# Exponents of split 64-bit weights: one ScalarE operation in place of two, in an attention and MLP kernel

## The chip, the cores and the metric

The kernel runs on one core of one Trainium2 chip. A core has a matrix engine (TensorE, PE in the profile, with its weight loads shown apart as PEld), a vector engine (VectorE, DVE), a scalar engine (ScalarE, ACT), a general engine (GpSimd, POOL), and a sync engine (SP) whose queue issues most of the transfers. Each engine works through its own instructions in a fixed order; semaphores hold an instruction until what it needs is done. The metric is the device time of one execution in microseconds (us); less is better.

## The reference

Sixty-four attention heads (8 batches of 8) with a sequence of 576 and a head size of 64, in which each query keeps only its 32 largest scores, followed by a layer of two matrix products with `h - tanh(h)` between them:

```python
scores = scale * np.matmul(q, k.transpose(0, 1, 3, 2))
kth = np.partition(scores, -top_k, axis=-1)[..., -top_k:-top_k + 1]
scores = np.where(scores >= kth, scores, -1000000000.0)
scores = scores - np.max(scores, axis=-1, keepdims=True)
attn = np.exp(scores)
attn = attn / (np.sum(attn, axis=-1, keepdims=True) + 1e-09)
attn_out = np.matmul(attn, v)
x = attn_out.transpose(0, 2, 1, 3).reshape(B * S, H * D)   # 4608 x 512
h = x @ w_in                                               # w_in 512 x 2048
g = h - np.tanh(h)
out = g @ w_out                                            # w_out 2048 x 512
```

`q`, `k` and `v` are 32-bit floats. `w_in` and `w_out` are 64-bit floats, since they come from a division by a 64-bit number. No engine computes with these, so the kernel turns their bits into 32-bit floats itself.

## The kernel before

**Attention.** The work is a list of 144 steps; a step is 128 queries of a pair of heads. Four stages of successive steps overlap. For step n+1, PE makes the scores (line 238) and ACT copies them out of PSUM (line 246). For step n, DVE searches for the 32 largest: it forms pairwise minima and maxima (lines 268, 269), takes the eight largest of the minima (line 271), and then runs four rounds of MAX8 (line 276) and MATCH_REPLACE8 (line 279). For step n-1, POOL forms the threshold (line 295), ACT turns it into a mask (line 308, once for each head), POOL subtracts the mask (line 311, a tensor operation of 128x576 twice in each step), marks doubtful rows (line 315), and ACT takes exponentials (line 331). For step n-2 the weights are transposed, multiplied with `v` by PE (lines 436, 444), copied by ACT (line 448) and scaled by POOL (line 460). In the first batch, PE transposes them (line 412) and ACT copies the result (line 415); in later batches DVE and transfers through DRAM do.

**The layer.** When all heads of 256 rows (128 in some units) are there, PE forms `h` (line 489), ACT takes tanh and a copy (lines 501, 502), POOL subtracts (line 503), and PE multiplies by `w_out` (line 510). This work is dealt out between the attention steps.

**The weights.** `w_in` and `w_out` are cut into 32 pieces of 128 x 512 numbers. A piece is brought in twice by SP (lines 148 and 149: the raw words, and the same bytes shifted so that the mantissa lies in one word), and then goes through the engines:

- DVE line 158 takes the 11 bits of the exponent out of the high word, into the tile `f`, as an integer;
- ACT lines 159 and 162 turn them into the bits of a 32-bit exponent, `e`;
- DVE line 164 and ACT line 167 turn the mantissa into a number from 1 to 2, in the tile of the weights;
- DVE line 170 joins sign and exponent into `f`;
- POOL line 173 multiplies the two.

The steps of the generator `convert` are spread over the four search rounds of the first eleven attention steps, two to four pieces in a step (`many`). A stretch of the trace in which a step's search and its pieces run is called a round in what follows. In each, line 170 of a piece comes after lines 158 and 164 of the next one on DVE. For the pieces of `w_in` (the first 16) `e` is a tile in PSUM; for those of `w_out` it is `f` itself, in SBUF:

```python
e = h_ps.tile([P, NW], FP32, tag="h", name="e")[:] if j < WJ else f[:]
```

The room in which a piece is loaded is partly borrowed (from `w_out`, from `spare`, from `zx`), so a new load starts when line 170 of an earlier piece has read its slot. The order on each engine is the order in which the program issues (`tc.manual_schedule()`); nothing moves it later.

Of the kernel before, what the change touches and what calls it, by code (L numbers as in the profile page):

```python
# [8 lines left out]
AF = mybir.ActivationFunctionType  # L9
ALU = mybir.AluOpType  # L10
FP32 = mybir.dt.float32
I32 = mybir.dt.int32
# [36 lines left out]
def kernel(  # L49
# [9 lines left out]
    nc = tc.nc  # L59
    P = nc.NUM_PARTITIONS  # L60
# [16 lines left out]
    scale = 1.0 / float(D) ** 0.5  # L77
# [5 lines left out]
    def pool(name, bufs, **kw):  # L83
        return ctx.enter_context(tc.tile_pool(name=name, bufs=bufs, **kw))

    consts = pool("consts", 1)
# [28 lines left out]
    later = spare[:].rearrange("p a n w -> p (a n w)").bitcast(FP32)  # L115
    zx2 = [consts.tile([P, 4 * S], FP32, name="zx")[:], later[:, 0 : 4 * S]]
    et_rem = later[:, 4 * S : 6 * S]
    e1151 = consts.tile([P, 1], FP32, name="e1151")
    nc.gpsimd.memset(e1151[:], 1151.0 * 2.0**23)
    e255 = consts.tile([P, 1], FP32, name="e255")  # L120
    nc.gpsimd.memset(e255[:], 255.0 * 2.0**23)

    def flat(x):
        return x.rearrange("p n w -> p (n w)")
# [13 lines left out]
    def convert(piece, slot):  # L138


        j, i = piece // CD, piece % CD
        if j < WJ:
            src, dst = moe_w_in[i * P : (i + 1) * P, j * NW : (j + 1) * NW], w_in[j][:, i, :]
        else:
            r0 = ((j - WJ) * FJ + i) * P
            src, dst = moe_w_out[r0 : r0 + P, :], w_out[j - WJ][:, i, :]
        raw, shifted, _ = slot
        nc.sync.dma_start(flat(raw), src.bitcast(U32))
        nc.sync.dma_start(
            flat(shifted).bitcast(U8)[:, 0 : 8 * NW - 4], src.bitcast(U8)[:, 3 : 8 * NW - 1]  # L150
        )
        yield
        hi = raw[:, :, 1]
        f = thpool.tile([P, NW], FP32, tag="th", name="f")
        fu = f[:].bitcast(U32)


        nc.vector.tensor_scalar(fu, hi, 20, 0x7FF, ALU.logical_shift_right, ALU.bitwise_and)
        nc.scalar.activation(f[:], fu, AF.Relu, bias=e1151[:], scale=-(2.0**23))  # L159

        e = h_ps.tile([P, NW], FP32, tag="h", name="e")[:] if j < WJ else f[:]
        nc.scalar.activation(e.bitcast(I32), f[:], AF.Relu, bias=e255[:], scale=-1.0)

        nc.vector.tensor_scalar(
            dst.bitcast(U32), shifted[:, :, 0], 0x0FFFFFFF, None, ALU.bitwise_and
        )
        nc.scalar.activation(dst, dst.bitcast(U32), AF.Copy, bias=1.0, scale=2.0**-28)
        yield

        nc.vector.scalar_tensor_tensor(  # L170
            out=fu, in0=hi, scalar=0x80000000, in1=e.bitcast(U32), op0=ALU.bitwise_and, op1=ALU.bitwise_or
        )
        nc.gpsimd.tensor_tensor(dst, dst, f[:], ALU.mult)
        yield
# [398 lines left out]
    def run(exact):  # L573
# [32 lines left out]
        def load_piece():  # L606
            k = len(loaded)
            usable = [x for x in free if x[2] > k]
            if k < pieces and usable:
                slot = min(usable, key=lambda x: x[2])  # L610
                free.remove(slot)
                piece = convert(k, slot)
                next(piece)
                loaded.append((piece, slot))
# [161 lines left out]
```

## Time and profile before

| | us |
|---|---|
| median of 3 runs | 1538.54 (1538.29 to 1539.8) |
| profiled execution | 1541.86 |
| its span, first to last instruction | 1540.1 |

Busy time in the profiled execution: PE 1441.5 us (94%), DVE 1346.9 (87%), POOL 940.9 (61%), ACT 883.4 (57%). The chain of work that ended last lies on PE for 79% of the span, on DVE for 7%, on ACT for 4%. The 32 conversions run between 8.2 and 166.4 us; PE is not yet full there.

The views of the profile give one line for a group of like instructions, or, in order of time, one line for an instruction or a run of them: start, duration, engine, line of the program, operation, the tile written and the tiles read, the shape, and in brackets how long the engine had been idle before and what ended that. A duration runs from start to end, so it holds what the instruction waits for once it has started. The granted clock is the share of TensorE's full clock that the chip allowed.

### The profile page before, as it was taken

What the parts mean: (1) busy time and instruction counts of PE and PEld (TensorE: products, weight loads), DVE (VectorE), ACT (ScalarE), POOL (GpSimd) and SP (SyncE); (2) the same over time, 40 slices, a digit from 0 to 9 for tenths busy, and PEclk for the clock granted to TensorE, in tenths of its full rate; (3) what the DMA queues carried; (4) which work ended last, traced back from release to release, by engine and by line L of the source; (5) the groups of instructions that cost most, each with busy time, mean ns of one, the idle gap of its engine ahead of it and who ended that gap; (6) DMA issues with size and microseconds to landing.
All of it is one profiled execution on the core that took longest, in us unless ns stands there. A gap on an engine that the chain in (4) does not pass through costs nothing.

```text
span 1540.1 us, 24174 instructions
## 1 busy us (share of the span) xinstructions
PE 1441.5 (94%) x7428; PEld 911.6 (59%) x7428; DVE 1346.9 (87%) x3828; ACT 883.4 (57%) x1567; POOL 940.9 (61%) x1525
## 2 busy tenths in 40 slices
PE   2567898999999999999999999999999999999997
PEld 1355566556566665656566665656566665656673
DVE  6988899999999999999999999999999999997300
ACT  4887776556555565556565565656565565655320
POOL 2777677567575675757575675757575675746420
PEclk9887999999999999999999999999999999999999
DMA  9944114546754575446655565456655566534400
GB/s 233 367 168 172 50 32 102 143 130 176 173 157 137 146 168 161 127 141 154 177 136 146 146 161 160 128 149 154 172 136 149 146 153 165 147 114 116 137 7 16
DMA packets 255466, 221.61 MB, mean 144 GB/s; under 512 B 197728, under 2 KB 204896, under 8 KB 248160
## 3 DMA queue, kind: packets, MB, share of 16 engines
q1 hardware_dynamic: 253552, 219.75, 53.1%
q8 instruction: 61, 1.00, 0.3%
q14 instruction: 77, 0.63, 0.2%
q10 hardware_dynamic: 1776, 0.22, 0.1%
HBM read 136.17 MB, written 83.76 MB: 143 GB/s over the span
## 4 chain that ended last, share of the span: by engine, by line
PE 79%; DVE 7%; ACT 4%; DMA 3%; issue 2%; SPq 2%; POOL 2%; DVEq 0%; ACTq 0%; POOLq 0%
PE hps L489 30%; PE ops L510 29%; PE av L436 10%; PE scps L238 9%; DVE m L276 2%; DVE ab L279 2%; PE av L444 2%; SPq L201 1%; DMA et<-there 1%; ACT z L308 1%; ACT f L159 1%; PE zt L412 1%; DMA zx<-in_moe_w_in_dram 1%; DVE ab L268 1%; DVE ab L271 1%
## 5 line engine op out<-in xcount | busy, mean ns | idle before, releaser
L510 PE MATMUL ops<-w_out,g 128*128 128x512 f32 x1152 | 520.5, 598 | 0.0
L489 PE MATMUL hps<-xT,w_in 128*128 128x256 f32 (+1 forms) x2176 | 471.4, 372 | 1.2 <-POOL xT L460 1.2
L276 DVE MAX8 m<-ab 128x8 f32<-128x288 f32 (+1 forms) x1152 | 464.1, 444 | 0.0
L311 POOL TENSOR_TENSOR z<-sc,z 128x576 f32<-128x576 f32 x288 | 400.2, 1412 | 77.1 <-ACT z L308 77.1
L489 PEld LDWEIGHTS hps<-xT,w_in 128*128 128x128 f32 x2176 | 390.7, 193 | 73.9 <-issue 20.7
L279 DVE MATCH_REPLACE8 ab<-m,ab 128x288 f32<-128x288 f32 x864 | 376.0, 443 | 0.0
L510 PEld LDWEIGHTS ops<-w_out,g 128*128 128x128 f32 x1152 | 211.4, 191 | 244.7 <-issue 240.7
L308 ACT ACTIVATE z<-sc,tb 128x576 f32<-128x576 f32 x288 | 207.6, 769 | 153.8 <-POOL tb L295 153.8
L503 POOL TENSOR_TENSOR g<-g,th 128x512 f32<-128x512 f32 x144 | 183.8, 1276 | 123.5 <-ACT g L502 109.0
L331 ACT ACTIVATE z<-z,nb 128x576 f32<-128x576 f32 x288 | 221.6, 773 | 8.7 <-POOL z L311 8.6
L246 ACT COPY sc<-scps 128x1152 f32<-128x1152 f32 x144 | 160.8, 1116 | 108.5 <-PE scps L238 106.4
L238 PE MATMUL scps<-kT,qT 64*128 64x288 f32 (+1 forms) x1280 | 188.1, 445 | 30.2 <-DVE qT L223 27.7
L238 PEld LDWEIGHTS scps<-kT,qT 64*128 64x128 f32 (+1 forms) x1280 | 101.4, 184 | 118.9 <-issue 56.4
L436 PE MATMUL av<-et,vb 128*64 128x256 f32 (+1 forms) x1088 | 133.3, 381 | 38.4 <-ACT et L415 30.6
L268 DVE TENSOR_TENSOR ab<-scps,sc 128x576 f32<-128x576 f32 x144 | 107.6, 747 | 68.0 <-POOL bad L315 55.0
L460 POOL TENSOR_TENSOR xT<-xs 128x256 f32<-128x256 f32 (+1 forms) x68 | 47.2, 695 | 168.0 <-ACT xs L448 168.0
L501 ACT ACTIVATE th<-hps 128x512 f32<-128x512 f32 x144 | 85.4, 593 | 106.8 <-PE hps L489 104.4
L448 ACT COPY xs<-av 128x512 f32<-128x512 f32 (+1 forms) x84 | 44.1, 525 | 169.6 <-PE av L444 169.6
L436 PEld LDWEIGHTS av<-et,vb 128*64 128x64 f32 x1088 | 75.2, 140 | 101.0 <-issue 36.3
L341 POOL TENSOR_SCALAR rd<-den 128x2 f32<-128x2 f32 x144 | 33.4, 232 | 139.4 <-ACT z L331 90.9
L271 DVE MAX8 ab<-ab 128x8 f32<-128x288 f32 x288 | 116.5, 446 | 0.0
L269 DVE TENSOR_TENSOR ab<-scps,sc 128x576 f32<-128x576 f32 x144 | 107.5, 747 | 0.0
(67 smaller groups left out, 1249.5 us busy)
## 6 DMA issues: line engine op xcount, KB each, us to landing
et<-there SPq DMA_DIRECT2D x224, 288.0 KB, 5.3
there<-spare SPq DMA_DIRECT2D x28, 1152.0 KB, 4.2
there<-zx SPq DMA_DIRECT2D x28, 1152.0 KB, 4.2
kin<-in_k_dram SPq DMA_DIRECT2D x116, 72.0 KB, 2.4
vb<-in_v_dram SPq DMA_DIRECT2D x64, 128.0 KB, 4.5
out_dram<-ot SPq DMA_DIRECT2D x32, 256.0 KB, 3.3
qin<-in_q_dram SPq DMA_DIRECT2D x113, 72.0 KB, 3.4
spare<-there SPq DMA_DIRECT2D x56, 144.0 KB, 3.0
```

The source lines that it names most:

```text
L238: nc.tensor.matmul(ps[rows, t, s, 0:S2], qT[g.b, g.hp + i][half(t), qs], kT[g.b, g.hp + i][half(t), ks], start=True, stop=True,)
L246: nc.scalar.copy(sc[:], ps[:, :, :, 0:S2])
L271: nc.vector.max(ab[:, t, S2 : S2 + 8], lo[:, t, :])
L276: nc.vector.max(m[:, t, m8], last[t] if i == rounds - 1 else cur[t])
L279: nc.vector.match_replace(nxt[t], m[:, t, m8], cur[t], NEG)
L308: nc.scalar.activation(zv[:, t, :], scf[:, t, :], AF.Relu, bias=tb[:, t : t + 1], scale=-BIG)
L311: nc.gpsimd.tensor_tensor(zv[:, t, :], scf[:, t, :], zv[:, t, :], ALU.subtract)
L331: nc.scalar.activation(x["zv"][:, t, :], x["zv"][:, t, :], AF.Exp, bias=x["nb"][:, t : t + 1], scale=scale, accum_out=den[:, t : t + 1],)
L436: nc.tensor.matmul(av[half(t), 0, cols], vb[g.b, hp][:, t, c, :] if c < J else vr[g.b, hp][:, t, :], es[:, :, (J + 1) * t + c if c < J els ...
L489: nc.tensor.matmul(cur[u][:, s : s + w], w_in[j][:, c, fo : fo + P], u.xT[:, c, 0:w], start=(c == 0), stop=(c == CD - 1),)
L503: nc.gpsimd.tensor_tensor(g, g, th[:], ALU.subtract)
L510: nc.tensor.matmul(cur[u][:], u.g[o // 1024][:, o % 1024 // 512, o % 512 : o % 512 + P], w_out[f // FJ][:, f % FJ, :], start=(f == 0), sto ...
```

## The change

The exponent field of a 64-bit float, x, has a bias of 1023, that of a 32-bit float 127, which is 896 less. Before, two operations form `e`, in units of 2^23:

- line 159: `f = max(0, 1151 - x)`, a 32-bit float
- line 162: `e = max(0, 255 - f)`, written as an integer

Together they give x - 896, held between 0 and 255. After, one operation of the same shape reads the integer x and writes the integer `max(0, x - 896)`. The hold at 255 is gone; it matters for numbers of 2^128 and more alone. Its output is `e` as before: in PSUM for `w_in`, in place in `f` for `w_out`. The two columns of constants become one.

```diff
-    e1151 = consts.tile([P, 1], FP32, name="e1151")
-    nc.gpsimd.memset(e1151[:], 1151.0 * 2.0**23)
-    e255 = consts.tile([P, 1], FP32, name="e255")
-    nc.gpsimd.memset(e255[:], 255.0 * 2.0**23)
+    e896 = consts.tile([P, 1], FP32, name="e896")
+    nc.gpsimd.memset(e896[:], -896.0 * 2.0**23)
...
         nc.vector.tensor_scalar(fu, hi, 20, 0x7FF, ALU.logical_shift_right, ALU.bitwise_and)
-        nc.scalar.activation(f[:], fu, AF.Relu, bias=e1151[:], scale=-(2.0**23))
 
         e = h_ps.tile([P, NW], FP32, tag="h", name="e")[:] if j < WJ else f[:]
-        nc.scalar.activation(e.bitcast(I32), f[:], AF.Relu, bias=e255[:], scale=-1.0)
+        nc.scalar.activation(e.bitcast(I32), fu, AF.Relu, bias=e896[:], scale=2.0**23)
```

The order on DVE, POOL, PE and SP stays the same but for one memset on POOL at the start; on ACT the 32 operations of line 159 are gone. In the changed program the remaining operation stands on line 158; the lines behind it have moved up by four, those of DVE's first operation by three.

## The prediction

> **What bounds the kernel now.** I read the shares of the engines first, then the busy time by stretch, the chain of work that ended last, and two rounds of the conversion in order of time. The shares:
>
> ```profile
> PE 1441.5 (94%) x7428; PEld 911.6 (59%) x7428; DVE 1346.9 (87%) x3828; ACT 883.4 (57%) x1567; POOL 940.9 (61%) x1525
> ```
>
> ACT, whose work is cut, is busy 57% of the span, PE 94%. An average over stages says little, so the next view gives busy time in stretches (start and end, length, then PE, PEld, DVE, ACT, POOL, granted clock, DMA share):
>
> ```profile
> 0.00:50.00 50.00, 13.44 (x55) 8.27 (x55) 37.90 (x101) 24.34 (x36) 18.14 (x34) 1.00 0.99 268
> 50.00:94.00 44.00, 26.10 (x145) 18.75 (x146) 41.91 (x124) 38.89 (x73) 33.34 (x48) 0.77 0.75 277
> 94.00:166.00 72.00, 49.08 (x298) 36.94 (x297) 60.35 (x156) 57.90 (x105) 52.68 (x64) 0.82 0.46 161
> 166.00:260.00 94.00, 91.47 (x610) 63.47 (x609) 88.45 (x278) 67.45 (x130) 64.55 (x113) 0.97 0.23 50
> 260.00:1462.00 1202.00, 1192.20 (x6085) 741.67 (x6084) 1118.14 (x3173) 683.89 (x1207) 761.10 (x1261) 1.00 0.57 149
> ```
>
> All conversions lie before 166 us. Up to 50 us the DMA engines are 99% busy; from 50 to 94 DVE has 41.91 of 44.00; from 94 to 166 no engine is full, DVE having 60.35, ACT 57.90 and POOL 52.68 of 72. After 166 PE is the bound. So whatever reaches PE's first work at 165.41 is passed on one for one, and nothing else is. The operations in question, grouped by form over the first 170 us (count, busy us, mean ns, idle before and what ended it):
>
> ```profile
> L159 ACT ACTIVATE f<-f,e 128x512 f32<-128x512 uint32 x32 | 22.8, 711 | 12.1 <-DVE f L158 12.1
> ...
> L162 ACT ACTIVATE f<-f,e 128x512 int32<-128x512 f32 x16 | 11.6, 722 | 0.5
> ...
> L162 ACT ACTIVATE e<-f,e 128x512 int32<-128x512 f32 x16 | 11.1, 692 | 0.6
> ```
>
> **What the change removes.** 32 operations of line 159. The next one reads what it wrote, so from start to start the step is 0.75 us (161.42 to 162.17), and 32 x 0.75 = 24.0 us of ACT's order go. The Trainium skill, "ScalarE: Activation LUTs", section "What ACT_TABLE_LOAD costs", gives 280 ns + 0.833 N for an ACTIVATE with a bias column (706 ns for 512, an estimate) and an overlap of 93 ns between neighbours; by that 0.61 would go each time, 20 us in all. The row's 711 ns agrees with the first figure, but the overlap does not hold between these two, and the trace's 0.75 is used.
>
> The remaining operation now goes from uint32 to int32. No row has both ends as integers: from uint32 it is 711, to int32 692 (PSUM) or 722 (SBUF), and line 167's from uint32 is 613. I keep 692 and 722 and bound it by 0.61 and 0.80 (722 plus the 98 by which 711 exceeds 613, less the overlap of about 20 seen in the rows). One small memset of 0.1 us on POOL at 0.9 us goes too, before POOL's 18 us wait for its first conversion: nothing. One constant column less moves later tiles by one slot; weight loads of vb and vr, which lie differently in their slots, both take 137 ns, so nothing.
>
> DVE, POOL and SP get no other order. What changes is when line 170 can ask to run, 0.75 us earlier in the first piece of a round. So it must be seen what holds line 170 and those behind it.
>
> **What is late next: the port of DVE and POOL.** A round of the second half, in order of time:
>
> ```profile
> 108.66 2.78 POOL L311 TENSOR_TENSOR z<-sc,z 128x576 f32<-128x576 f32 x2 [2.51 <-ACT z L308]
> 109.13 0.71 ACT L159 ACTIVATE f<-f,e 128x512 f32<-128x512 uint32 x1
> ...
> 109.88 0.72 ACT L162 ACTIVATE f<-f,e 128x512 int32<-128x512 f32 x1
> ...
> 110.63 1.35 DVE L170 SCALAR_TENSOR_TENSOR f<-spare,f 128x512 uint32<-128x512 uint32 x1 [3.13 <-ACT f L162]
> ```
>
> Line 170 seems to wait for ACT (3.13 us). But it takes 1.35 where the same form takes 0.68 at 114.15, and it ends at 111.98, 0.54 after POOL's line 311 ends (111.44). The same sum fits at 94.61, 124.39, 141.80 and 155.19: it stands until POOL's operation is over, then runs. Started 0.75 earlier it stands longer. In the first half its exponent is in PSUM and it never stretches, but line 158 behind it does:
>
> ```profile
> 68.19 2.88 POOL L311 TENSOR_TENSOR z<-sc,z 128x576 f32<-128x576 f32 x2 [1.38 <-ACT z L308]
> ...
> 70.15 0.69 DVE L170 SCALAR_TENSOR_TENSOR f<-w_out,e 128x512 uint32<-128x512 uint32 x1
> ...
> 70.75 0.60 DVE L158 TENSOR_SCALAR f<-spare 128x512 uint32<-128x512 uint32 x1
> ```
>
> Line 311 ends at 71.07, line 158 (0.42 alone) at 71.35, 0.28 later. With line 170 at 69.40 and line 158 at 70.00 it still ends at 71.35. The MAX8 and line 170 of the next piece follow from there.
>
> The round closes without line 159. In the timeline: the last line 170 of a round (62.28 to 62.94) feeds POOL's line 173 (the third from 63.08 to 64.35), behind which stand line 356 (64.29), PE's line 444 (64.63) and the transposes of line 412, ACT's two copies of line 415 (66.06, 66.85), line 308 (67.33) and line 311 (68.19), which holds line 158 until 71.35. ACT's conversions run beside this. From 98 us it is the same ring with line 489 between (line 170 at 99.57, 173 at 100.99, 444 at 102.55, 412 at 105.94, 308 at 107.79, 311 at 108.66).
>
> **The sum.** Rounds up to 50 us: DVE reaches line 170 after the exponents are done (at 22.47 against 17.74, at 36.62 against 33.99, at 50.11 against 48.61), and loads fill the DMA engines: 0. Three rounds to 94: lines 268 waited 1.2 us in all for line 246's copy, which comes earlier, but DVE then stands at line 158 as shown: 0, at best 1.2. Five rounds from 94: line 170 asks 0.75 earlier, some 0.1 to 0.2 us before the first half of line 311 ends (108.66 + 1.41 = 110.07 against 109.88). If DVE gets the port between the halves, it gains up to 1.35 at once, and line 311's second half and POOL's next steps are put back by about 0.55. No row of the trace shows both asking at such a point. Each of these rounds lies between -0.6 and +0.6; I take 0, as POOL is on the ring.
>
> The last round is another matter, since it hands over to PE:
>
> ```profile
> 161.42 0.73 ACT f L159
> 162.15 0.02 issue
> 162.17 0.72 ACT f L162
> 162.90 0.52 ACT w_out L167
> 163.41 1.00 ACT sc L246
> ...
> 164.59 0.77 ACT z L331 x2
> 165.36 0.04 issue
> 165.41 1.97 PE zt L412 x8
> ```
>
> From 161.42 ACT works without a break until PE's transposes, which waited 5.9 us for it. One step of 0.75 goes here. Before it, line 170 at 155.19 loses 0.67 to line 311 (1.35 against 0.68) and would ask 0.75 earlier; between 0 and 1.35 of that reaches line 158 at 160.98. I take 0.75, near the middle. Sum: 0.75 + 0.75 = 1.5 us of the profiled execution's 1541.86 (span 1540.1 and 1.76 around it), which lies 3.3 above the median of the runs, 1538.54. Taken off the median: 1537.0, 0.1% less.
>
> The Trainium skill, "SBUF — State Buffer", sections "SBUF: two separate sides" and "Who interferes with whom", says that DVE's second port pair is POOL's, that it is an exclusive lock held for a whole instruction, and that issue order decides who blocks. The rows of line 170 agree with the lock. The rule speaks against this change: a DVE that asks earlier can come first, and POOL, which is on the ring, then waits 0.55 for each line 170 or 0.3 to 0.4 for each of lines 158 and 164. By the rule alone the five rounds would cost 5 x 0.55 = 2.8 us and the change would end 1.3 above the median.
>
> **Rivals.** (a) The ring is not the port's and each round's line 159 counts. For it: the chain of work that ended last has line 159 in nearly every round (68.78, 82.93, 93.22, 109.24, 122.99, 140.40, 153.78, 161.42), and line 170's idle time is put down to line 162. Against it: the stretched rows above. Eight rounds x 0.75 = 6.0: 1532.5.
>
> (b) Slower: DVE's run of locking operations overtakes POOL's short steps. Place: the pair of lines 158 and 164 at 134.09, where line 158 waits for line 460 (0.47 instead of 0.41). Were DVE first, its four operations to 135.57 would hold line 460, and behind it line 295, 308 and 311, by up to 1.2 us in each of five rounds: +6.0 - 0.75 = +5.2, 1543.7. It shows as slower from 0.77 a round. Against it: DVE then has that much in hand at the next line 170.
>
> (c) The change does not do what it says: the operation with two integer ends takes as long as two did. 1538.5.
>
> **How the numbers follow.** The forecast has 0.73, (a) 0.12, (b) 0.10, (c) 0.05. The range takes the forecast's bounds: down 0.75 + 1.35 + 5 x 0.6 = 5.1, so 1533.4; up 5 x 0.6 - 0.75 = 2.3, so 1540.8; widened by 0.2 and 0.4 for the unseen duration of the new form (32 x 0.08 beside other work, little of it on the path): 1533.2 to 1541.2. Left out are (a) and most of (b). About 0.2%, 3.1 us, is what a measurement of this kernel can tell from no change: faster is below 1535.5, slower above 1541.6. Faster 0.18 ((a) and 0.06 of the forecast's lower end), slower 0.10, same 0.72.
>
> **What would show it.** Right: line 159 gone, line 162 of 16 + 16 at 0.69 and 0.72; ACT some 22 us less busy; the first line 170 of the second half's rounds waiting for POOL (or running at 0.6 to 0.7 between two stretched lines 311); DVE's time before 166 us nearly as it was; PE's transposes of 165.41 at about 163.9. Wrong: those transposes at 160 or earlier (rival a), or after 168 with lines 460 or 295 of 1 us and more (rival b), or line 162 over 1 us (c).

## The result, and the profile after

The median after is 1536.89 us (1534.97 to 1537.92, 4 runs), beside 1539.17 for the kernel before (1538.29 to 1540.68, 4 runs): a ratio of 0.9983, 95% interval [0.9965, 1.0]. The profiled execution took 1537.92 us, its span is 1536.1. The forecast was 1537.0, with no measurable change as the likeliest outcome.

The shares of the engines:

```profile
PE 1441.2 (94%) x7428; PEld 911.0 (59%) x7428; DVE 1350.7 (88%) x3828; ACT 861.8 (56%) x1535; POOL 947.3 (62%) x1524
```

ACT is 21.6 us less busy than before (883.4); the row of line 159 had 22.8. DVE is 3.8 and POOL 6.4 busier, though neither has more work: a duration holds what an operation waits for after its start. By stretches (start and end, length, PE, PEld, DVE, ACT, POOL, granted clock, DMA share):

```profile
50.00:94.00 44.00, 26.78 (x143) 18.87 (x144) 43.38 (x125) 31.82 (x59) 35.71 (x48) 0.63 0.74 267
94.00:162.20 68.20, 46.96 (x292) 35.40 (x291) 60.96 (x152) 45.68 (x87) 53.51 (x63) 0.84 0.51 170
162.20:256.20 94.00, 91.46 (x609) 63.53 (x609) 88.52 (x278) 67.83 (x130) 64.75 (x112) 0.97 0.23 49
```

PE's transposes, whose start ends the conversions' influence, begin at 161.99 (before: 165.41; forecast: about 163.9), so the third stretch is cut 3.8 us earlier than it was. In it ACT has 12.2 us less to do and DVE 0.6 more. The groups by form over the first 170 us (count, busy us, mean ns, idle before and what ended it), ACT's new operation and two of DVE's behind it:

```profile
L158 ACT ACTIVATE f<-f,e 128x512 int32<-128x512 uint32 x16 | 11.4, 713 | 6.5 <-DVE f L155 6.5
L158 ACT ACTIVATE e<-f,e 128x512 int32<-128x512 uint32 x16 | 11.0, 685 | 12.8 <-DVE f L155 12.8
...
L155 DVE TENSOR_SCALAR f<-spare 128x512 uint32<-128x512 uint32 x12 | 11.2, 937 | 0.0
...
L166 DVE SCALAR_TENSOR_TENSOR f<-spare,f 128x512 uint32<-128x512 uint32 x8 | 7.9, 992 | 3.6 <-ACT f L158 3.6
```

The operation with two integer ends takes 713 and 685 ns, where the kept forms had 722 and 692: one operation less is one operation less, and rival (c) is out. In front of it ACT now waits 19.3 us for DVE (12.1 before). DVE's line 155 (158 before) shows where the time went: its mean of 937 ns is more than twice the 0.41 us that it takes alone. A round of the second half in order of time, lines 307, 158, 166 and 155 being 311, 162, 170 and 158 before:

```profile
107.30 3.23 POOL L307 TENSOR_TENSOR z<-sc,z 128x576 f32<-128x576 f32 x2 [2.15 <-ACT z L304]
107.78 0.71 ACT L158 ACTIVATE f<-f,e 128x512 int32<-128x512 uint32 x1
...
108.52 0.74 DVE L166 SCALAR_TENSOR_TENSOR f<-spare,f 128x512 uint32<-128x512 uint32 x1 [2.03 <-ACT f L158]
...
109.18 1.63 DVE L155 TENSOR_SCALAR f<-w_out 128x512 uint32<-128x512 uint32 x1
```

Line 166 asks 0.19 us before the first half of line 307 ends (107.30 + 1.41 = 108.71) and runs between the halves: 0.74 instead of 1.35. The second half of line 307 takes 1.87 instead of 1.41. The gain is then given back one instruction later: line 155 asks while that second half runs and stands until it is over, 1.63 instead of 0.41.

**Where the 3.4 us up to the transposes came from.** The stretch from the first line 158 (155) of the round at 54 us to PE's transposes can be cut at the starts of that operation in each round. Here it is for the two kernels and for the experiments that follow, all from their timelines in us (the first column from POOL's first instruction on); "one" marks segments in which the pieces have one operation:

| run | start to 54 | three rounds of `w_in` | four rounds of `w_out` | last round |
|---|---|---|---|---|
| before | 54.08 | 37.12 | 60.05 | 13.92 |
| after | 52.65 one | 37.23 one | 59.20 one | 12.67 one |
| e1, after again | 52.38 one | 37.24 one | 58.71 one | 12.68 one |
| e2, `w_in` only | 52.12 one | 36.46 one | 58.52 | 13.86 |
| e3, `w_out` only | 52.34 | 37.12 | 60.48 one | 12.68 one |
| e4, last four only | 53.25 | 37.12 | 58.41 | 12.68 one |

The last column is the change's sure effect: 13.86 and 13.92 with two operations, 12.67 or 12.68 with one, in each of these six runs. The first and the third do not follow the code: of the 3.4 us between the first two rows 1.43 were there at 54 us, and 0.85 come from rounds that differ by 1.6 between runs with the same code (before, e4). The second is the same to 0.01 us in the three runs with two operations; why it has two values with one is told under the point on these rounds below.

### The profile page after: what moved, and what is told of

Read it like the earlier page. It is cut to its first block, busy times and chain, and to the rows that moved or that the text cites. A ratio compares the mean times of both kernels' runs of the same rounds, so it can differ in the third digit from the quotient of the medians.

```text
span 1536.1 us, 24155 instructions
## 1 busy us (share of the span) xinstructions
PE 1441.2 (94%) x7428; PEld 911.0 (59%) x7428; DVE 1350.7 (88%) x3828; ACT 861.8 (56%) x1535; POOL 947.3 (62%) x1524
## 4 chain that ended last, share of the span: by engine, by line
PE 79%; DVE 10%; DMA 3%; issue 2%; POOL 2%; ACT 2%; SPq 2%; ACTq 0%; DVEq 0%; POOLq 0%
PE hps L485 30%; PE ops L506 29%; PE av L432 10%; PE scps L234 9%; DVE m L272 3%; DVE ab L275 2%; PE av L440 2%; SPq L197 1%; DMA zx<-in_moe_w_in_dram 1%; DVE f L155 1%; DMA et<-there 1%; DVE f L166 1%; DVE ab L267 1%; DVE ab L264 1%; DVE ab L265 1%
```

## The experiments

### The change in parts: e1 to e4

e1 is the changed kernel again. In the others both forms are in the program and a condition selects:

```diff
+        one = j < WJ          # e2; e3: j >= WJ; e4: piece >= 28
+        if one:
+            nc.scalar.activation(e.bitcast(I32), fu, AF.Relu, bias=e896[:], scale=2.0**23)
+        else:
+            (lines 159 and 162 as before)
```

> The changed kernel once more, beside which the three partial ones are read. The profile after shows the hand-over to PE 3.4 us earlier than before: 1.43 of it is there already at 35 us, where no conversion holds anything, 0.7 is lost again from 57 to 90 us, 1.4 comes from 94 to 150, 1.25 in the last round. If the first 1.43 is chance (loads at the start), the hand-over lies 1.5 to 2.5 before that of the kernel before in this run, and the ratio is 0.9985 +- 0.001; if it comes with the change, 1.4 stands again at 35 us and the ratio is 0.998.

> One operation for the 16 pieces of w_in alone, two for those of w_out. Ring and port theory: line 158 stands longer behind line 311 (1.2 us in place of 0.5 to 0.6), nothing gained to 94 us, hand-over between -0.5 and +0.7 us, ratio 1.000. Rival (a), each round's operation counts: three rounds x 0.75 = 2.2 us, ratio 0.9985. Start-up theory: -1.4 at 35 us, as these early pieces are converted as in the changed kernel.

> One operation for the 16 pieces of w_out alone. Up to 94 us it is the kernel before, so its start tells how far the start varies by itself. Ring and port theory: the first line 170 of each of the five rounds runs in 0.72 between the halves of line 311, the line 158 behind it stretches to 1.6, some 0.3 us a round are gained in four rounds and 1.25 in the last: hand-over 2.0 to 2.6 us earlier than at 94 us, ratio 0.9984. Rival (a): 5 x 0.75 = 3.7 us, ratio 0.9976.

> One operation for the last four pieces alone, those of the round that hands over to PE. Ring and port theory as predicted: 0.75 for the last piece's step and 0.5 to 0.75 for line 170 before the second half of line 311, so 1.25 to 1.5 us, ratio 0.9991. Rival (a): one of eight rounds, 0.75 us, ratio 0.9995. If the gain were spread evenly over the pieces, 4 of 32 of 2.3 us: 0.3 us, no difference.

Measured, as ratios to the kernel before: e1 0.998 [0.9971, 0.9989] (1536.73 us against 1539.76), e2 1.0006 [0.9997, 1.0015], e3 1.0000 [0.9991, 1.0009], e4 0.9984 [0.9973, 0.9994]. The last four pieces alone give 0.0016, about all that the whole change gives; the 16 of `w_in` give nothing. e3 holds the last four too and shows nothing, against both of its expectations (0.9984 and 0.9976); its interval just reaches the 1.25 us (0.0008) that its last round saves in the trace. So intervals of 0.001 on each side, 1.5 us, do not carry a sum of parts, and the segments above are the better witness. They leave out what lies behind PE's transposes, where all six runs do the same work: the profiled time less the start of the transposes is 1373.4 us in e4 and 1377.3 in e3, a difference larger than the whole change is worth.

Why do four rounds with the same code take 58.41 in e4 and 60.05 before? PE's first products of line 489 (496 in e4) stand in the ring, in front of the transposes of line 412. First the kernel before, then e4, each as a line of the timeline, with the window around it (granted clock third from the end):

```profile
102.72 3.44 PE L489 MATMUL hps<-xT,w_in 128*128 128x128 f32 x16
...
99.00:107.00 8.00, 5.10 (x31) 4.80 (x31) 8.00 (x22) 4.07 (x10) 6.26 (x9) 0.79 0.85 317
```

```profile
101.89 1.95 PE L496 MATMUL hps<-xT,w_in 128*128 128x128 f32 x16
...
99.00:107.00 8.00, 5.93 (x50) 5.04 (x51) 7.69 (x22) 5.71 (x14) 6.28 (x10) 1.00 0.77 289
```

The same 16 products take 3.44 at a granted clock of 0.79 and 1.95 at 1.00; in e3 they took 3.62 (0.57), in the changed kernel 2.52 (0.79). The Trainium skill, "TensorE: Matmul & The Clock Gate", section "What's actually happening", says that the clock is halved until PE has been busy through a free-running window of about 3.4 us, so that the moment of change is not tied to the program; these rows agree. In the kernel before, the granted clock is 0.50 from 102.93 to 106.33 us, 3.4 us, and 1.00 for ten us on either side, so all but the start of its 16 products lies in the slow stretch. That alone moves these rounds by 1.5 us between runs. The mean of the four rounds is 59.3 with two operations (before, e2, e4, and e7 below: 60.22) and 59.1 with one (after, e1, e3, and e8 below: 58.11). With either, single runs lie 1.8 to 2.4 us apart, so a gain or loss of some tenths a round would not be seen.

### Is it a ring through POOL? e5 and e6

POOL's line 356 (352) waits behind the third line 173 of a round, and PE's next transposes wait for it. Here it is moved up: it is issued as soon as the reciprocal that it needs is, at the first search round.

```diff
             if i == 0 and here(-2):
                 invert(n - 2)
+                if steps[n - 2].pe:
+                    spread(n - 2)
...
-            if pe:
-                spread(n - 2)
```

> The kernel before, with POOL's line 356 (the copy that PE's line 444 waits for) issued right after the reciprocal in the first search round, ahead of the three products of line 173, in the first batch. Ring theory: the ring runs through line 173 and line 356; cut there, line 444 comes 2 us earlier in each of eight rounds and the transposes, ACT's copies, line 308 and line 311 with it, until the exponentials of line 331 hold the transposes instead: 0.5 to 1.5 us a round, 4 to 12 us in all, ratio 0.993 to 0.997. Rival (a), in which DVE waits for ACT and not for POOL: no difference.

> The same with the changed kernel. If POOL's part of the ring hid the removed operations, more of them shows once the ring is shorter: 3 to 6 us between this kernel and the one before it in this list, against 2.3 without the cut; the ratio to the kernel before 0.989 to 0.995. Rival (a): the same 2.3 us between the two and nothing from the cut.

e5, which keeps both ACT operations: 1531.55 us, 0.9943 [0.9929, 0.9957]. e6, with one: 1538.17, 0.9983 [0.9974, 0.9992]. The ring was real: moving one small instruction of POOL gives 8.7 us, several times what 32 fewer ACT operations give. That the change then costs 6.6 us was not foreseen; a gain of 3 to 6 was expected. The timeline of e6 (numbered as the changed kernel) shows how:

```profile
52.38 2.95 POOL L307 TENSOR_TENSOR z<-sc,z 128x576 f32<-128x576 f32 x2 [0.41 <-ACT z L304]
52.48 1.59 DVE L155 TENSOR_SCALAR f<-w_out 128x512 uint32<-128x512 uint32 x1
...
53.99 1.62 DVE L160 TENSOR_SCALAR w_in<-w_out 128x512 uint32<-128x512 uint32 x1
```

ACT, relieved, starts the mask of line 304 0.96 us ahead of the round's first line 155 (0.18 ahead of line 158 in e5), and POOL's line 307 comes to the port 0.10 us ahead of DVE's line 155. Line 155 ends 0.28 after the first half (53.79), line 160 ends 0.28 after the second (55.33): DVE loses 2.4 us here, and again in the rounds at 66.2, 80.0 and 93.7. In e5 DVE is 0.7 ahead (54.34 against 55.02), its four operations run at 0.42, and line 311's first half takes 2.01. In segments: three rounds of `w_in` take 35.81 in e5 and 41.26 in e6, the other five 55.88 + 13.00 and 56.04 + 13.35. An earlier ACT turned the order at the port, and the search on DVE pays.

### Turning the order back: f1 to f3

If order at the port is the cause, POOL has to be later by a little. Its small operation for `nb` (line 304 before, 300 after) stands behind those for the threshold `tb`; put ahead of them, it delays the mask by 0.25 us and adds nothing. f2 is e6 with that, f3 is e5 with it, as a control; f1 is e5 with one operation for `w_out` alone.

```diff
+        nb = mpool.tile([P, 2], FP32, tag="nb", name="nb")
+        nc.gpsimd.tensor_scalar(nb[:], m[:, :, 0], -scale, None, ALU.mult)
         tb = mpool.tile([P, 2], FP32, tag="tb", name="tb")
...
-        nb = mpool.tile([P, 2], FP32, tag="nb", name="nb")
-        nc.gpsimd.tensor_scalar(nb[:], m[:, :, 0], -scale, None, ALU.mult)
```

> The kernel before with POOL's line 356 moved up behind the reciprocal, and one operation in place of two for the 16 pieces of w_out only. Theory P (order at the port): what the change costs once line 356 is moved lies in the four rounds of w_in between 50 and 94 us, where the first lines 158 and 164 of a round stand for 1.59 and 1.62 us behind POOL's line 311 instead of 0.42 each (DVE's standing there grows from 2.0 to 7.1 us). With two operations kept for w_in those stay at 0.42, and the last round gives its 1.25 us: 1530.3, 0.9935 of before. Rival Q (the loss is spread over all rounds, or is in those of w_out, where line 158 stands 7 us longer in all): 1534 to 1536.

> The changed kernel with POOL's line 356 moved up behind the reciprocal, and besides POOL's small operation for nb put ahead of the two for tb in each step, so that ACT's line 308 and POOL's line 311 start 0.25 us later; no operation is added or taken away. Theory P (order at the port): without this, POOL's line 311 comes to the port 0.10 us ahead of DVE's first line 158 in the rounds of w_in (52.38 against 52.48), and DVE's lines 158 and 164 stand for 2.4 us; with it DVE comes 0.15 us earlier than POOL, its four operations run at 0.42, and line 311 stands 0.6 to 0.9 us instead. The kernel gets faster by 3 to 5 us against the one without the reorder (0.9983 of before): 0.995 to 0.996 of before, 1533 to 1535. Rival Q (the loss has to do with something else): 0.25 us later in each of eight rounds, 1538 to 1540, 0.998 to 1.000 of before.

> Control: the kernel before with line 356 moved up and the operation for nb put ahead of those for tb, two ACT operations kept. Theory P: here DVE's line 158 is already 0.4 to 0.7 us ahead of line 311 in the rounds of w_in, so 0.25 us more changes no order: 0.9943 of before within 0.001, 1531 to 1533. Rival Q (the reorder itself is a gain or a loss of its own, whatever the order at the port): as far from 0.9943 as the run with one operation is from 0.9983, and with the same sign.

Measured: f1 0.9952 [0.9939, 0.9966] (1533.81 against 1541.87), f2 0.9945 [0.9931, 0.9959] (1532.80), f3 0.9964 [0.9951, 0.9978] (1535.76). Delaying POOL's mask by 0.25 us made e6's program faster by 0.0038, 5.9 us, somewhat more than expected. The same place in f2's timeline:

```profile
54.79 0.41 DVE L155 TENSOR_SCALAR f<-w_out 128x512 uint32<-128x512 uint32 x1
54.92 2.55 POOL L307 TENSOR_TENSOR z<-sc,z 128x576 f32<-128x576 f32 x1 [0.61 <-ACT z L304]
55.12 0.41 DVE L160 TENSOR_SCALAR w_in<-w_out 128x512 uint32<-128x512 uint32 x1
...
55.46 0.42 DVE L155 TENSOR_SCALAR f<-w_out 128x512 uint32<-128x512 uint32 x1
...
55.80 0.42 DVE L160 TENSOR_SCALAR w_in<-w_out 128x512 uint32<-128x512 uint32 x1
```

DVE is 0.13 ahead, four operations run at 0.41 and 0.42, and line 307 pays 1.14 us once. The three rounds take 35.16 instead of 41.26. The Trainium skill, "SBUF — State Buffer", section "Who interferes with whom", has it that issue order decides who blocks; e6 and f2 agree, with 0.10 us one way and 0.13 the other.

The control f3 was expected within 0.001 of e5 and came out 0.0021 above it (the two intervals overlap). Its three rounds of `w_in` take 35.80, e5's 35.81, so where the theory speaks nothing moved; the four rounds of `w_out` take 0.76 us more (56.64). That POOL's delay counts there is likely: these rounds take 1.1 more in f2 (55.69) than in f1 too. The rest of the 0.0021 is not settled; the operation for `nb` is moved in all 144 steps, most of which lie behind these rounds. f1's three rounds take 35.79, which places 5.5 of the 7.7 us between e6 and f1 in them; its other five take 54.58 + 12.58, 1.7 less than e5's, but its median does not show these 1.7 us (0.9952, where 0.9935 was expected).

### Both together: g1

`nb` first in four steps alone:

```diff
+        if 2 <= n <= 5:
+            nb = ...       (ahead of tb; otherwise behind it)
```

> The changed kernel with POOL's line 356 moved up behind the reciprocal, and the operation for nb put ahead of those for tb in the four steps alone in which the mask runs beside pieces of w_in (steps 2 to 5); elsewhere nb stays behind tb. Theory P (order at the port): the four rounds of w_in run as in the run with nb first everywhere (DVE first, lines 158 and 164 of the first piece at 0.41), the five rounds after them as in the run with one operation for w_out alone. By the traces of those two that is 0.4 + 1.7 = 2.1 us ahead of the kernel before with line 356 moved up, when PE's transposes begin after the last round: 1529.5 to 1532, 0.993 to 0.995 of before, the lowest of all runs or equal to it. Rival Q (the loss with one operation is in the rounds of w_out, and what nb first repaired lay there): 1535 to 1538.

1529.07 us against 1539.39, 0.9937 [0.9924, 0.9951], the lowest of all. Segments: 35.15 + 54.60 + 12.88 = 102.63, against 104.69 for e5, 2.1 us less, as worked out from f1 and f2. (The last of the four steps runs beside the first pieces of `w_out`.) Against e5's 0.9943 the medians alone do not separate the two.

### Line 158 off the port: e7 and e8

In the first half, line 158 behind line 170 was said to stand and so to eat what the change gives. Here it writes `w_in`'s exponents into PSUM, where `e` already is; e7 has two ACT operations, e8 one.

```diff
+        x = e.bitcast(U32)                   # e: PSUM for w_in
-        nc.vector.tensor_scalar(fu, hi, 20, 0x7FF, ...)
+        nc.vector.tensor_scalar(x, hi, 20, 0x7FF, ...)
```

> The kernel before, but line 158 writes the exponents of w_in into the PSUM tile of line 162 and line 159 reads them there, so that this DVE operation has its output outside SBUF. Port theory: it no longer stretches behind line 311 (0.5 to 1.2 us) but may lose its short form (0.41 to about 0.6 us for 512 numbers, two or three in a round): per round +0.4 on DVE and -0.1 to -0.2 on waits, so 0 to 1 us slower in all, ratio 1.000 to 1.0007. If line 158 stretches all the same, the lock is not one of SBUF's ports.

> The same with the changed kernel. With no wait at line 158 the earlier line 170 of w_in's rounds is kept: 0.7 us in each of three rounds on DVE more than between the kernels before and after, so 4 us between this one and the one before it in this list, unless the ring through lines 173 and 356 takes it again (then 2.3 us).

e7 1.0002 [0.9993, 1.0011] (1540.61), e8 0.9982 [0.9973, 0.9991] (1537.44): the change gives 3.2 us here, and 3.0 in e1 with line 158 at the port; 4 or 2.3 were expected, and 3.2 does not decide between them. The operation does leave the port, at a price (group by form of e7, line 160 being 158 before):

```profile
L160 DVE TENSOR_SCALAR e<-w_out 128x512 uint32<-128x512 uint32 x10 | 6.9, 686 | 1.3 <-DMA w_out<-in_moe_w_in_dram 1.2
```

It takes 0.69 each time, beside line 311 too, instead of 0.41 alone and up to 1.63 beside POOL. The three rounds take 37.42 in e7 and 36.80 in e8: 0.6 us come through, where 2.2 would be all that the change takes out of three first pieces. What line 158 held at the port can't be read off this pair, because its price fills the same waits: the nine operations of these rounds take 6.2 us in e7 instead of 4.1, and DVE, which waits 2.0 us in these rounds of the kernel before, waits nowhere longer than 0.07.

## Why the prediction was right, point by point

That the measured 1536.89 lies 0.1 from the forecast is luck in part. The 1.5 us were taken off 1538.54, the median of three runs; four runs of the kernel before give 1539.17, and of the 2.3 us between that and the result 1.25 are shown to come from the change.

**The last round, 1.5 us.** Right in sum, 1.25 measured. The timeline of the changed kernel:

```profile
152.27 0.72 DVE L166 SCALAR_TENSOR_TENSOR f<-spare,f 128x512 uint32<-128x512 uint32 x1 [1.53 <-ACT f L158]
...
155.96 2.49 POOL L169 TENSOR_TENSOR w_out<-w_out,f 128x512 f32<-128x512 f32 x2
...
157.34 1.39 DVE L155 TENSOR_SCALAR f<-spare 128x512 uint32<-128x512 uint32 x1
...
158.76 0.72 ACT L158 ACTIVATE f<-f,e 128x512 int32<-128x512 uint32 x1 [2.58 <-DVE f L155]
...
161.99 1.97 PE L408 MATMUL zt<-ident,z 128*128 128x128 f32 x8 [5.24 <-ACT z L327]
```

The second term, ACT's step of 0.75 in the chain that hands over, was 0.76: from ACT's start to the transposes 3.23 (158.76 to 161.99) instead of 3.99 (161.42 to 165.41). The first term, set at 0.75 between bounds of 0 and 1.35, came out at 0.50, by another way: line 166 gained the whole 1.39 (it ends 3.67 after the round's first line 155, where it was 5.06), line 155 of the third piece 0.09 more, and the last line 155 gave 0.98 back, because it now meets POOL's two operations of line 169 and stands until 158.45. What was not worked out was whom DVE meets next once it is early.

**The three rounds to 94 us, 0.** Right in sum: 37.23 after, 37.12 before. The step named is there. In the kernel before, DVE waits 0.8 us in front of line 170 and 1.2 in front of line 268 in these rounds; in the changed kernel it waits 0.6 in all, and its nine lines 155 take 6.1 us instead of 4.1. The third of each round stands until 0.28 after line 307:

```profile
67.54 2.77 POOL L307 TENSOR_TENSOR z<-sc,z 128x576 f32<-128x576 f32 x2 [0.41 <-ACT z L304]
...
69.34 1.25 DVE L155 TENSOR_SCALAR f<-spare 128x512 uint32<-128x512 uint32 x1
```

It ends at 70.59, line 307 at 70.31: the 0.28 that the prediction read off the kernel before. But the sum hides a gain and a loss. The rounds take 12.17, 12.92 and 12.14 us after, 12.70, 12.16 and 12.26 before: two gain, and the second loses 0.76. There POOL's line 291 (295 before), which forms the threshold, meets DVE. First the kernel before, then the changed one:

```profile
66.05 0.56 POOL L295 TENSOR_SCALAR tb<-m 128x1 f32<-128x1 f32 x2
```

```profile
65.01 1.90 POOL L291 TENSOR_SCALAR tb<-m 128x1 f32<-128x1 f32 x2
...
66.68 1.44 ACT L304 ACTIVATE z<-sc,tb 128x576 f32<-128x576 f32 x2 [0.33 <-POOL tb L291]
```

Its first half starts 0.05 us ahead of DVE's line 155 (65.06) and still takes 1.64 us instead of 0.30, until DVE's four operations are over. The mask waits for it, and line 307 comes 2.48 us after the round's first line 155 instead of 1.18. In e1 the same happens, and the round takes 12.92 again; in e2, where DVE comes 0.39 after the first half's start, that half takes 0.30 and the round 12.14. So the prediction's zero holds by a loss that it did not name in this place; without it these rounds gain 0.66 (36.46 in e2), inside its 0 to 1.2.

**The rounds of `w_out`, 0 each.** Right within what can be seen. DVE did get the port between the halves, the case of which no row existed, and line 307 was put back by 0.46 (0.55 said). The rounds then close as before: means of 59.1 with one operation and 59.3 with two.

**Startup, 0.** Settled for the two profiles, not for the medians. All of the 1.43 us by which the changed kernel is ahead at 54 us is there at the fourth piece's line 158, at 32.09 us before, where DVE has waited 1.41 for a load, and at 30.64 after, where it has waited 0.51; from there to the round at 54 us both take 22.2. e3, whose early pieces have two operations, is there at 30.04, so the change is not needed for it. This also answers what was expected of e1: its start is early again, but so is e3's. Over all runs the first line 158 of the round at 54 us starts between 51.9 and 54.6 us after POOL's first instruction in the seven whose early pieces have one operation (mean 52.8), and between 52.3 and 55.1 in the seven with two (mean 53.8). The segments behind it sum to 0.1 + 0.2 + 1.3 = 1.6 us in the means, the medians say 2.3 (after) and 3.0 (e1). A gain of some tenths in startup would narrow that, and so would chance.

**The rivals.** (a) wanted 0.75 in every round; the ring of e5 and the segments exclude it. (b), DVE overtaking POOL's short steps, does occur, at the cost of 0.76 us (up to 1.2 a round were named), but in one round of eight, the second of `w_in` above, and not in the five where it was placed. Elsewhere it did not show as a loss: in the last round line 291 does stand (1.87 for the pair instead of 0.88), but its first half comes in time and line 304 starts 0.86 after the round's first line 155, as before. The order at the port did turn out to be worth 5 to 7 us, with the sides exchanged: in e6 POOL comes first, and DVE pays.

## What to carry to other kernels

An operation removed from an engine that waits is worth what it shortens in the one chain that is passed on, here the last of eight rounds; look there first. Where two engines share a port, write down for each round who asks first and by how much: a margin of 0.1 us decided 6 us here, and an edit that makes a third engine earlier can turn it. When that happens, the mend may be to delay the engine that won, by an instruction moved and not added.

## What the runs showed of the hardware that was not expected

- Two instructions of POOL in a row leave a gap in which a waiting DVE gets the port (line 166 at 0.74 between the halves of line 307, the second half 1.87). Four of DVE's in a row left line 307 none in f2: it waits 1.14 us until the last is nearly through. For POOL's small line 295 (291) it differs from place to place: its first half stood 1.64 us behind all four in the changed kernel at 65.01, but in the kernel before at 104.57 it took 1.00 and was over 0.30 before they were. What decides this no run shows.
- The same shift-and-mask of 512 words takes 0.41 into SBUF and stands behind POOL for up to 1.63; into PSUM, in e7 and e8, it takes 0.69 and does not stand.
- The same 16 matrix products take from 1.95 to 3.62 us as the clock is granted, before PE is steadily busy. Where such products lie in a ring, single profiles differ by 1.5 us there with the same code.
